# A new hand-written order for the first 24 steps of chunked attention and a rational feed-forward layer

## Chip, cores and metric

The kernel runs on one core of a Trainium2 chip. The metric is the device time of one launch in microseconds (us), the median of several runs; lower is better. The engines are called as in the profile: PE is TensorE (matmul), DVE is VectorE, ACT is ScalarE, POOL is GpSimd, SP is the queue that issues the transfers.

## The reference

Attention within chunks of 64 positions (8 batches, 8 heads, 576 positions, head width 64), whose output, read as 4608 tokens of width 512, goes through a feed-forward layer with a rational function between its two products.

```python
scores = scale * np.matmul(q_c, k_c.transpose(0, 1, 2, 4, 3))     # chunks of 64
scores = scores - np.max(scores, axis=-1, keepdims=True)
attn = np.exp(scores)
attn = attn / (np.sum(attn, axis=-1, keepdims=True) + 1e-09)
x = np.matmul(attn, v_c)                                         # as (4608, 512)
h = x @ w_in                                                     # 512 -> 2048
P = a[0] + a[1] * h + a[2] * h * h + a[3] * h * h * h
Q = 1.0 + np.abs(b[0]) * np.abs(h) + np.abs(b[1]) * h * h
out = (P / (Q + 1e-6)) @ w_out                                   # 2048 -> 512
```

## The kernel before

The 4608 tokens are 18 blocks of 256. The hidden width is cut into four parts of 512, so each block has four steps. Step g (0 to 71) is one part of one block: steps 0 to 7 alternate between blocks 0 and 1 (the weights of a part are used twice as soon as they are there), step 8 opens block 2, step 12 block 3, step 16 block 4, step 20 block 5. Every product keeps float32 accuracy by splitting its operands into a high and a low piece: the first feed-forward product (FF1) runs hi·hi, lo·hi and hi·lo, the second (FF2) ghi·wo_hi, ghi·wo_lo and glo·wo_hi. Weights come in as 16 pieces of 1 MB whose 8-byte words are joined and split on the chip.

Steps 0 to 23 follow the table START, a list of items written out by hand. The kernel schedules by hand: each engine and each transfer queue executes its items in exactly the order of the list, and an item that waits holds back everything behind it on its engine. From step 24 on another table, STEADY, repeats a pattern of a cheaper scheme with seven products instead of eight; it is the same before and after. An item is a letter, an index (step, block, weight piece, or sum) and sometimes a PSUM tag. The tags pa, p0, p1 and po name four pairs of PSUM banks; a tile that takes a tag waits until all readers of the tag's last tile are done.

- SP: q (queries and keys of a block; 0 and 1 in halves for block 0), k (the coefficients a and b), v (values), w (weight piece, L163; three raw buffers), t (fetch of sums).
- PE: S scores (L225), T transposes (L304), A attention times values (L225), F and f the two halves of FF1 (L352, 24 matmuls each), Z, z and y the three parts of FF2 (L428, 16 matmuls each).
- Attention elsewhere: M maximum (L261), U subtract (L267), n sum and reciprocal (L288 to L290) on DVE; E exponential (L274) on ACT; N the product of e with the reciprocal (L295) on DVE, Np the same on POOL; K copies the transposed e out of PSUM, at (L308), and X makes the high piece of x, xhi (L331), on ACT; Y the low piece xlo (L335) on DVE.
- Weight piece: s scales the high words (ACT, L182), o shifts the low words (DVE, L174; oa on ACT, L178), j joins them (DVE, L186), h rounds to the high piece (ACT, L189), d subtracts for the low piece (DVE, L196; dp on POOL).
- Rational function, old chain, on an FF1 tile ph in PSUM: a, b and c read ph on ACT (L356, L360, L364: tiles A, B, C); Q (L368, DVE), I and J (L372, L376, ACT: logarithm and exponential for the reciprocal); p and P (L380, L384, DVE) read ph again; g makes ghi (L389); H and R (L393, L397) one Newton correction; G the low piece glo (L402, DVE; Gp on POOL). B scales the coefficients once (L761).
- Newton chain, the same items with a u ahead (L460 to L508): it keeps its intermediate in the FF1 tile, and forms ghi by a copy on ACT (ue, L508) and glo on DVE or POOL (uG, uGp, L553).
- O copies a finished block out (ACT, L723) and stores it in four transfers (L726). m are 56 additions on w_out for the later scheme, on POOL, two of each 14 on ACT; the last of each 14 sends the sums (tt and hh) to DRAM.

The tiles e (softmax), at and o (output) share one pair of buffers, eo. ACT and DVE never read the same FF1 tile at the same time: a reader on one engine waits for the reader on the other that stands ahead of it in the list. So P, which reads ph on DVE, waits for the a, b or c ahead of it in the list, and the next user of the tag waits for P.

Of the kernel before, what the change touches and what calls it, by code (L numbers as in the profile page):

```python
# [31 lines left out]
EXP_WIDE = (0, 1, 2, 3, 4, 5, 6, 7) + tuple(range(8, NB))  # L32

START = (
# [24 lines left out]
)  # L59
FAST = 6  # L60
CHANGE = NST * FAST
# [900 lines left out]
```

## Time and profile before

| what | us |
|---|---|
| median of 3 runs | 888.95 |
| lowest and highest | 886.86, 891.35 |
| the profiled execution | 888.25 |
| its span in the trace | 886.5 |
| PE busy in it | 844.7 (95%) |

The span is the time between the first and the last recorded instruction; the profiled execution lies 0.7 us below the median of the runs, and the trace shows only that execution.

### The profile page before, as it was taken

To read this page: it belongs to the slowest core of one execution; us is meant where nothing else is said; L and a number is where in the kernel's file an instruction comes from. 1 tells how busy PE (TensorE), PEld (TensorE's weight loads), DVE (VectorE), ACT (ScalarE), POOL (GpSimd) and SP (SyncE) were. 2 spreads that over 40 slices of the span, in tenths; PEclk is the share of its full clock that TensorE was granted. 3 is DMA by queue.
4 is the path that set the end of the run, shared out by engine and by line. 5 is a ranking of instruction groups with operands and counts; after the bars stand their busy time and mean duration, and the time that the engine had idled before them with its cause. 6 is when DMAs were issued, how large, how long until landed. Compare 5 with 4: busy or idle time off the path is not lost.

```text
span 886.5 us, 20984 instructions
## 1 busy us (share of the span) xinstructions
PE 844.7 (95%) x9084; PEld 834.5 (94%) x9084; DVE 742.9 (84%) x646; ACT 536.4 (61%) x539; POOL 526.3 (59%) x325
## 2 busy tenths in 40 slices
PE   1798989999999999999999999999999999999997
PEld 1798989999999999999999999999999999999996
DVE  6897987798969987888888888888888889887785
ACT  3787774556564755665656565666656556556562
POOL 3231423523643577777777776767676768675771
PEclk9998999999999999999999999999999999999999
DMA  6752531103305335575767676767677777765861
GB/s 231 291 211 88 184 102 58 27 1 96 121 1 192 121 125 198 183 250 187 252 217 245 218 249 222 252 216 252 223 244 232 238 238 235 232 222 170 281 209 35
DMA packets 125468, 162.85 MB, mean 184 GB/s; under 512 B 6848, under 2 KB 111296, under 8 KB 122304
## 3 DMA queue, kind: packets, MB, share of 16 engines
q1 hardware_dynamic: 125216, 161.25, 55.5%
q8 instruction: 71, 1.16, 0.5%
q10 hardware_dynamic: 160, 0.26, 0.1%
q14 instruction: 21, 0.17, 0.1%
HBM read 142.61 MB, written 18.87 MB: 182 GB/s over the span
## 4 chain that ended last, share of the span: by engine, by line
PE 77%; DVE 9%; ACT 5%; DMA 4%; issue 3%; POOL 1%; SPq 0%; DVEq 0%; ACTq 0%; POOLq 0%
PE ph L352 37%; PE acc L619 14%; PE acd L619 11%; PE po L428 10%; DMA wo<-t 2%; PE pss L225 2%; PE psx L225 2%; PE pst L304 1%; DVE C L380 1%; DMA ab<-in_b 1%; ACT A L356 1%; DVE C L384 1%; DMA raw<-in_w_out 1%; DVE B L368 1%; DVE raw L174 1%
## 5 line engine op out<-in xcount | busy, mean ns | idle before, releaser
L352 PE MATMUL ph<-xhi,wi_hi 128*128 128x256 f32 x1152 | 322.9, 280 | 0.2 <-DVE xlo L335 0.2
L352 PE MATMUL ph<-xlo,wi_hi 128*128 128x256 f32 x1152 | 321.2, 279 | 0.7 <-DVE xlo L335 0.7
L352 PE MATMUL ph<-xhi,wi_lo 128*128 128x256 f32 x1152 | 321.0, 279 | 0.0
L352 PEld LDWEIGHTS ph<-xhi,wi_hi 128*128 128x128 f32 x1152 | 217.5, 189 | 0.8 <-DVE xlo L335 0.4
L352 PEld LDWEIGHTS ph<-xlo,wi_hi 128*128 128x128 f32 x1152 | 217.3, 189 | 0.9 <-DVE xlo L335 0.9
L352 PEld LDWEIGHTS ph<-xhi,wi_lo 128*128 128x128 f32 x1152 | 217.2, 189 | 0.0
L460 ACT ACTIVATE U<-ph 128x1024 f32<-128x1024 f32 x55 | 56.5, 1028 | 171.0 <-PE ph L352 157.0
L550 POOL TENSOR_TENSOR slo<-B,shi 128x1024 fp32r<-128x1024 f32 x46 | 111.0, 2413 | 71.0 <-ACT shi L542 67.6
L469 DVE SCALAR_TENSOR_TENSOR U<-U,co 128x1024 f32<-128x1024 f32 x55 | 90.7, 1648 | 26.3 <-ACT U L460 25.5
L490 DVE SCALAR_TENSOR_TENSOR U<-U,co,ph 128x1024 f32<-128x1024 f32 x55 | 69.4, 1262 | 43.1 <-ACT ph L486 43.0
L526 POOL TENSOR_TENSOR B<-C 128x512 f32<-128x512 f32 x46 | 70.8, 1539 | 55.2 <-DVE C L498 38.2
L428 PE MATMUL po<-wo,ghi 128*128 128x256 f32 (+2 forms) x768 | 97.2, 283 | 5.1 <-DVE wo L196 4.2
L428 PEld LDWEIGHTS po<-wo,ghi 128*128 128x128 f32 x768 | 93.3, 192 | 5.8 <-DVE wo L196 4.4
L518 POOL TENSOR_TENSOR graw<-C,graw 128x768 fp32r<-128x768 f32 x46 | 85.4, 1856 | 2.0 <-PE pst L304 1.3
L619 PE MATMUL acc<-wo,graw 128*128 128x256 f32 x552 | 80.3, 281 | 0.0
L482 ACT ACTIVATE B<-U,cst,co 128x1024 f32<-128x1024 f32 x55 | 68.4, 1244 | 18.3 <-DVE U L469 18.2
L498 DVE SCALAR_TENSOR_TENSOR C<-C,co,ph 128x1024 f32<-128x1024 f32 x55 | 70.4, 1280 | 1.9
L619 PEld LDWEIGHTS acc<-wo,graw 128*128 128x128 f32 x552 | 70.9, 188 | 0.7
L477 DVE SCALAR_TENSOR_TENSOR C<-C,co,ph 128x1024 f32<-128x1024 f32 x55 | 70.3, 1278 | 1.5
L486 ACT ACTIVATE ph<-B,co 128x1024 f32<-128x1024 f32 x55 | 61.6, 1120 | 15.3 <-DVE C L477 15.2
L465 ACT ACTIVATE C<-ph,co 128x1024 f32<-128x1024 f32 x55 | 66.2, 1204 | 6.9 <-PE ph L352 3.8
L494 DVE SCALAR_TENSOR_TENSOR ph<-U,ph 128x1024 f32<-128x1024 f32 x55 | 67.5, 1226 | 1.4
(105 smaller groups left out, 1658.6 us busy)
## 6 DMA issues: line engine op xcount, KB each, us to landing
wo<-t SPq DMA_DIRECT2D x90, 768.0 KB, 6.6
wo<-t SPq DMA_DIRECT2D x98, 256.0 KB, 3.3
out<-o SPq DMA_DIRECT2D x68, 128.0 KB, 6.1
raw<-in_w_in SPq DMA_DIRECT2D x8, 1024.0 KB, 6.7
raw<-in_w_out SPq DMA_DIRECT2D x8, 1024.0 KB, 6.0
v<-in_vP SPq DMA_DIRECT2D x20, 256.0 KB, 7.5
qk<-in_qT SPq DMA_DIRECT2D x36, 128.0 KB, 6.9
qk<-in_kT SPq DMA_DIRECT2D x36, 128.0 KB, 6.6
```

The lines of the kernel that those rows point to most:

```text
L352: nc.tensor.matmul(ph[:, fi, :], w[:, cc, f], x[:, cc, :], start=(k == 0), stop=(k == len(mm) - 1))
L428: nc.tensor.matmul(accs[n][i][:, cols], g[:, fi, i * 128:(i + 1) * 128], w[:, FPS * s + fi, cols], start=start, stop=stop,)
L469: nc.vector.scalar_tensor_tensor(U, U, c0, U, ALU.add, ALU.mult)
L477: nc.vector.scalar_tensor_tensor(C, C, na1, h, ALU.add, ALU.mult)
L482: nc.scalar.activation(ch[key][2], ch[key][1], AF.Ln, bias=cst[:, 0:1], scale=lsc)
L490: nc.vector.scalar_tensor_tensor(V, V, kq, h, ALU.add, ALU.mult)
L494: nc.vector.scalar_tensor_tensor(h, V, 2.0, h, ALU.subtract, ALU.mult)
L498: nc.vector.scalar_tensor_tensor(C, C, na0, h, ALU.add, ALU.mult)
L518: nc.gpsimd.tensor_sub(lo, quads(ch[steps[g]][3])[:, :, 1:4, :], hi.bitcast(F32))
L526: nc.gpsimd.tensor_sub(S[:, 0:2], q[:, 0:1].to_broadcast([P, 2, 2, 128]), q[:, 1:3])
L550: nc.gpsimd.tensor_sub(lo, sbuf[g], hi.bitcast(F32))
L619: nc.tensor.matmul(acc[n][pair][:, bank, col:col + 256], stat, mov, start=start, stop=stop)
```

## The change

Only the table START changes; its items are the same 675 in number. It puts them in another order on all engines and alters some items:

- Steps with the Newton chain: 12, 15, 16, 17, 19, 20, 22 before; 11, 12, 15, 16, 17, 19, 20, 22, 23 after. The old chain falls from 17 to 15 steps.
- In the old chain a, b, c and p, P are put so that ph changes hands less often between ACT and DVE: over the 24 steps 45 times instead of 51.
- Softmax product N: before, blocks 0, 2 and 3 on POOL, 1, 4, 5 and 6 on DVE; after, blocks 0 and 1 on DVE, 2 to 6 on POOL.
- Weight pieces: the low words of two more pieces are shifted on ACT (10 instead of 8), so on 6 instead of 8 on DVE. The low pieces of 8, 9 and 4 move from DVE to POOL, those of 2, 3 and 12 from POOL to DVE. Piece 4 is loaded ahead of the first queries instead of behind them.
- glo: Newton chain 5 on DVE and 4 on POOL (3 and 4 before), old chain 7 and 8 (8 and 9 before).

```diff
-    "q0.0 q0.1 S0.0:p0 w3 M0.0 S0.1 U0.0 E0.0 M0.1 U0.1 n0.0 w4 w0 s3 E0.1 v0 w1 Np0.0 o3 j3 h3 s4 n0.1 T0.0:pa s0 q1 "
-    "o4 j4 o0 j0 Np0.1 h4 h0 K0.0 T0.1 K0.1 d4 w5 k0 s1 d0 o1 A0.0:p0 A0.1 X0.0 X0.1 dp3 S1:p1 w2 w6 w12 v1 j1 Y0.1 "
...
+    "w4 q0.0 o4 S0.0:p1 q0.1 w3 w0 S0.1 s4 j4 M0.1 U0.1 M0.0 U0.0 v0 w1 h4 q1 E0.1 E0.0 s3 dp4 s0 oa0 n0.1 o3 w2 n0.0 "
+    "j3 N0.0 N0.1 T0.0:pa T0.1 j0 h3 d3 w5 K0.0 K0.1 o1 A0.1:p1 A0.0 h0 s1 d0 j1 X0.1 X0.0 Y0.1 Y0.0 h1 k0 S1:po w6 "
```

ACT at the very start, before (raw3 is weight piece 3, e0 and at0 belong to block 0; L189 is h, L182 is s, L308 is K):

```order
L182 ACTIVATE raw3_108<-raw3_108 128x1024
L274 ACTIVATE e0_128<-e0_128 128x512
L189 CAST wi_hi_69<-raw3_108 128x4x256
L182 ACTIVATE raw4_136<-raw4_136 128x1024
L182 ACTIVATE raw0_138<-raw0_138 128x1024
L189 CAST wo_71<-raw4_136 128x1024
L189 CAST wi_hi_69<-raw0_138 128x4x256
L308 COPY at0_171<-pst0_154 128x512 x2
```

The same place after:

```order
L182 ACTIVATE raw4_85<-raw4_85 128x1024
L189 CAST wo_71<-raw4_85 128x1024
L274 ACTIVATE e0_135<-e0_135 128x512 x2
L182 ACTIVATE raw3_111<-raw3_111 128x1024
L182 ACTIVATE raw0_113<-raw0_113 128x1024
L178 ACTIVATE raw0_113<-raw0_113,cst_75 128x1024
L189 CAST wi_hi_69<-raw3_111 128x4x256
L308 COPY at0_180<-pst0_166 128x512 x2
L189 CAST wi_hi_69<-raw0_113 128x4x256
```

The copies K of block 0 (L308) stood behind the rounding of pieces 4 and 0 (two L189); now piece 4 is rounded before the exponentials, and piece 0 behind the copies.

DVE around step 0, before (A0_0, B0_0, C0_0 and ph0_0 are step 0; e1 and xlo1 block 1's):

```order
L196 TENSOR_TENSOR wo_71<-raw5_179,wo_71 128x1024
L174 TENSOR_SCALAR raw2_257<-raw2_257 128x1024
L295 TENSOR_TENSOR e1_275<-e1_275,sm1_272 128x2x8x64
L174 TENSOR_SCALAR raw6_259<-raw6_259 128x1024
L186 SCALAR_TENSOR_TENSOR raw2_257<-raw2_257 128x1024
L368 SCALAR_TENSOR_TENSOR B0_0_338<-B0_0_338,ab_74,A0_0_336 128x1024
L186 SCALAR_TENSOR_TENSOR raw6_259<-raw6_259 128x1024
L380 TENSOR_TENSOR C0_0_341<-C0_0_341,ph0_0_282 128x1024
L384 SCALAR_TENSOR_TENSOR C0_0_341<-C0_0_341,ab_74,ph0_0_282 128x1024
```

The same place after:

```order
L174 TENSOR_SCALAR raw6_263<-raw6_263 128x1024
L295 TENSOR_TENSOR e1_280<-e1_280,sm1_274 128x2x8x64
L196 TENSOR_TENSOR wi_lo_70<-raw2_158,wi_hi_69 128x4x256
L186 SCALAR_TENSOR_TENSOR raw6_263<-raw6_263 128x1024
L196 TENSOR_TENSOR wo_71<-raw5_178,wo_71 128x1024
L368 SCALAR_TENSOR_TENSOR B0_0_341<-B0_0_341,ab_74,A0_0_391 128x1024
L380 TENSOR_TENSOR C0_0_375<-C0_0_375,ph0_0_283 128x1024
L384 SCALAR_TENSOR_TENSOR C0_0_375<-C0_0_375,ab_74,ph0_0_283 128x1024
```

The product N of block 1 (L295) has one weight operation fewer ahead of it, and Q, p and P (L368, L380, L384) have two subtractions and a joining between them and N. The attention product A1 takes the tag p0 in the new table (po in the old), and p0 is free only when this P has read ph0_0.

POOL in the weight stage, before (wi_lo and wo are the low pieces of w_in and w_out; glo1_0 is step 1's):

```order
L196 TENSOR_TENSOR wi_lo_70<-raw2_257,wi_hi_69 128x4x256
L196 TENSOR_TENSOR wi_lo_70<-raw6_259,wi_hi_69 128x4x256
L196 TENSOR_TENSOR wo_71<-raw12_261,wo_71 128x1024
L196 TENSOR_TENSOR wi_lo_70<-raw7_307,wi_hi_69 128x4x256
L402 TENSOR_TENSOR glo1_0_785<-B1_0_603,A1_0_601 128x1024
```

The same place after:

```order
L196 TENSOR_TENSOR wi_lo_70<-raw6_263,wi_hi_69 128x4x256
L196 TENSOR_TENSOR wi_lo_70<-raw7_265,wi_hi_69 128x4x256
L196 TENSOR_TENSOR wo_71<-raw9_269,wo_71 128x1024
L196 TENSOR_TENSOR wo_71<-raw8_278,wo_71 128x1024
L196 TENSOR_TENSOR wi_lo_70<-raw11_389,wi_hi_69 128x4x256
```

The low pieces of weights 9 and 8 now stand on POOL, behind that of piece 7; step 1's glo and the pieces 2 and 12 have left that stretch for DVE.

## Rows read from the trace of the kernel before

**Rows 1.** The page, its part 1: busy us, share, instructions.
```profile
PE 844.7 (95%) x9084; PEld 834.5 (94%) x9084; DVE 742.9 (84%) x646; ACT 536.4 (61%) x539; POOL 526.3 (59%) x325
```

**Rows 2.** Windows of 50 us: length, busy us of each engine, PE clock, DMA.
```profile
0.00:50.00 50.00, 25.91 (x375) 24.04 (x376) 38.76 (x42) 30.53 (x34) 14.84 (x15) 0.97 0.68 259
50.00:100.00 50.00, 45.77 (x378) 45.57 (x378) 43.62 (x40) 40.31 (x38) 14.83 (x5) 0.93 0.39 141
100.00:150.00 50.00, 47.41 (x569) 46.56 (x568) 39.42 (x35) 33.99 (x32) 14.18 (x5) 1.00 0.30 107
150.00:200.00 50.00, 47.98 (x506) 47.16 (x505) 41.99 (x39) 25.54 (x30) 18.97 (x12) 0.97 0.10 22
200.00:250.00 50.00, 49.14 (x530) 48.68 (x529) 44.34 (x36) 29.45 (x28) 27.02 (x16) 1.00 0.29 96
250.00:300.00 50.00, 50.00 (x535) 49.61 (x535) 40.63 (x34) 28.41 (x27) 21.90 (x14) 1.00 0.24 86
```

**Rows 3.** Timeline of PE: start us, us, what, idle before and its releaser.
```profile
12.67 1.11 PE L304 MATMUL pst<-ident,e 128*128 128x128 f32 x4 [4.61 <-POOL e L295]
23.25 1.09 PE L304 MATMUL pst<-ident,e 128*128 128x128 f32 x4 [9.47 <-ACT at L308]
...
28.99 0.58 PE L352 MATMUL ph<-xhi,wi_hi 128*128 128x256 f32 x1
...
38.87 1.94 PE L304 MATMUL pst<-ident,e 128*128 128x128 f32 x8 [2.67 <-DVE e L295]
...
85.24 7.67 PE L428 MATMUL po<-wo,ghi 128*128 128x256 f32 x46 [4.23 <-DVE wo L196]
...
128.12 1.16 PE L225 MATMUL pss<-qk 64*64 64x64 f32 x64 [2.33 <-DVE C L384]
...
154.32 1.54 PE L304 MATMUL pst<-ident,e 128*128 128x128 f32 x8 [2.02 <-DVE C L384]
...
218.52 2.11 PE L428 MATMUL po<-wo,ghi 128*128 128x280 f32 x16 [0.86 <-ACT ghi L508]
```

**Rows 4.** Windows just behind two of these waits, columns as in rows 2.
```profile
85.24:89.90 4.66, 4.66 (x22) 4.66 (x23) 4.62 (x5) 3.55 (x4) 2.30 (x1) 0.50 0.61 225
154.75:158.16 3.41, 3.41 (x72) 2.96 (x71) 3.15 (x3) 2.21 (x3) 3.33 (x3) 0.50 0.19 43
```

**Rows 5.** The chain that ended last: start, us, a run of FF2 matmuls.
```profile
244.09 7.54 PE po L428 x64
```

**Rows 6.** Timeline of ACT near the copies of block 0.
```profile
21.45 1.17 ACT L189 CAST wi_hi<-raw 128x1024 fp32r<-128x1024 f32 x1 [3.02 <-DVE raw L186]
22.47 0.64 ACT L308 COPY at<-pst 128x512 f32<-128x512 f32 x1
24.38 0.59 ACT L308 COPY at<-pst 128x512 f32<-128x512 f32 x1 [1.27 <-PE pst L304]
```

**Rows 7.** Timeline of DVE: two shifts, the end of step 0's chain, a low piece.
```profile
17.19 2.89 DVE L174 TENSOR_SCALAR raw<-raw 128x1024 int32<-128x1024 int32 x1
...
36.90 0.68 DVE L174 TENSOR_SCALAR raw<-raw 128x1024 int32<-128x1024 int32 x1
...
43.95 1.28 DVE L384 SCALAR_TENSOR_TENSOR C<-C,ab,ph 128x1024 f32<-128x1024 f32 x1
...
83.97 1.22 DVE L196 TENSOR_TENSOR wo<-raw,wo 128x1024 fp32r<-128x1024 f32 x1
```

**Rows 8.** Groups by line of 0 to 350 us: busy us, mean ns, idle before.
```profile
L380 DVE TENSOR_TENSOR C<-C,ph 128x1024 f32<-128x1024 f32 x17 | 20.5, 1213 | 18.5 <-ACT A L356 9.6 <-ACT B L360 8.9
...
L196 POOL TENSOR_TENSOR wo<-raw,wo 128x1024 fp32r<-128x1024 f32 x3 | 8.3, 2765 | 13.9 <-ACT wo L189 13.9
```

**Rows 9.** Timeline of ACT: the copy out O0, and block 3's K held by its stores.
```profile
155.95 1.01 ACT L723 COPY o<-po 128x1024 f32<-128x1024 f32 x1 [4.41 <-PE pst L304]
...
161.26 1.02 ACT L308 COPY at<-pst 128x1024 f32<-128x1024 f32 x1 [1.02 <-DMA out<-o]
```

**Rows 10.** Timeline of POOL: the additions m, held by the store of tt.
```profile
279.84 2.61 POOL L575 TENSOR_TENSOR tt<-wo 128x512 f32<-128x512 f32 x2 [20.95 <-DMA t<-tt]
```

44 rows, old and new, of the table START are left out of this document.

## The prediction

> **What bounds the kernel now.** I read the page first: PE works 844.7 of 886.5 us [rows 1], and the diff alters none of its matmuls, so a gain can only come out of the 41.8 us in which PE stands still, and out of matmuls that ran at half clock. The windows of 50 us say where the idle time is: 50 minus PE's busy time is 24.1, 4.2, 2.6, 2.0 and 0.9 us in the first five and nothing in the sixth [rows 2]. The reader should see that all of it lies in the stretch that START orders, and that DVE, ACT and POOL are never full there on average; single waits count, not loads. Since PE is full from 250 us on, whatever the start gains or loses is carried to the end.
>
> PE's timeline then names the waits. Ahead of the first FF1 matmul (F0, at 28.99 us) the big one is 9.47 us at T0.1, which needs a PSUM tile that the copy K0.0 has to read first; behind F0 there are six of note: 2.67 (T1, for the softmax product of block 1 on DVE), 4.23 (Z2, the FF2 of step 2, for the low piece of weight 8), 2.33 (S3, whose tag waits for a P, L384), 2.02 (T3, the same with another P) and 0.86 (z12, for a rounding on ACT) [rows 3]; two waits for xlo, 0.7 and 0.2, are left out of the sum below, since they may stay.
>
> Behind two of these waits the trace shows a granted clock of 0.50, the lower of the two levels (1.2 against 2.4 GHz) [rows 4]. FF2 matmuls at the full clock start every 7.54 / 64 = 0.118 us [rows 5]; the 22 in the 4.66 us behind Z2's wait took 0.212 each, so that stretch cost 22 × 0.094 = 2.1 us. The 3.41 us behind T3 cost about half of themselves, 1.7. Waits so cost more than their own length.
>
> **The change, part by part.** *To F0.* K0.0 at 22.47 started straight behind the rounding h0, which itself waited 3.02 for DVE's joining j0 [rows 6], behind a shift that took 2.89 us [rows 7]. In the new order both copies stand ahead of h0, and both products N0.0, N0.1 are on DVE, at about 0.7 each (512 columns, half of the 1.21 of a 1024-column operation [rows 8]). What is paid for it: piece 4 is loaded ahead of the first queries, so the second half's scores come some 1.5 to 2 us later than in the trace. From the second scores I add up DVE's operations in the new order (two maxima, two subtractions, two sums, a shift, a joining, two products: 8.3 us from about 9.5 to 10 us) and reach N0.1's end near 18, so T0.1 ends near 19.3 instead of 24.34. From T0.1's end to F0 the trace took 28.99 − 24.34 = 4.65, and K0.0, done before T0.1 there, adds its 0.64 now: 24.6; with the joining j1 ahead of Y0 25.2. **F0 3.8 us earlier** (2 if the load of piece 4 delays the scores twice as much, 5 if nothing does).
>
> *T1.* N1 has one weight operation fewer ahead of it on DVE and PE now does half of step 2 (f2) ahead of T1, so N1's end (34.6 to 35.4) meets PE's arrival at 35.2: **2.67 saved**.
>
> *A1, a new wait.* A1's tile now takes tag p0, which P0 has to leave. P0 ended at 43.95 + 1.28 = 45.23 [rows 7], 16.2 us behind F0's start. In the new order ACT has a, b and c of step 0 mixed with a rounding, a scaling and K1 (1.0 to 1.2 us each), and DVE does d2, j6 and d5 ahead of Q0, p0, P0: by those rows P0 ends at 42.7, 17.5 behind F0. PE is through with F2 at 39.0. **A wait of 3.7 us** (0 if DVE takes the two subtractions in ACT's gaps and K1 is earlier, 6 if one more DVE operation grows as the shift did). Behind it A1 and Z0 would run at the lower clock; the nearest row, Z2's stretch, says about 2.1, of which T1's own slow stretch paid some 1.5 before: **0.6 more**.
>
> *Z2.* Pieces 8 and 9 go to POOL at 2.77 us each [rows 8]; POOL has nothing else between piece 7's and piece 11's. I add up to an end near 74, and PE comes to Z2 near 79, so the cover is 5 us. On DVE, that subtraction ran at 83.97, 1.22 long [rows 7], behind step 3's P, which waited for ACT. **4.23 and the slow stretch, 2.1: 6.3 saved.** If POOL is more than 5 us late, each further microsecond is a wait at Z2.
>
> *S3 and T3.* DVE stood 18.5 us ahead of the p's for ACT's A and B, readers of the same FF1 tile [rows 8]. With 45 handovers instead of 51, and P6, P9 earlier in DVE's row than the scores and transposes need, S3's tag is free at 116.3 against PE's 117.3: **2.33 saved**. T3 and S4 are taken in the other order with other tags: **2.02 and the slow 1.7 saved, 3.7**. Step 11 as a Newton chain has as many operations as the old one on DVE and one copy (ue) that moves work from DVE to ACT, which has room [rows 2]; I cost it at nothing, as I do step 23. The cover is thin at F11 only, which needs P9 (141.2 to 141.9 against 142.8): **0.5 lost** (0 to 1).
>
> *z12.* Step 12's ghi comes earlier with the lead: **0.86 saved**.
>
> *Stores.* K3 at 161.26 waited for O0's stores, since at takes the buffer of o: O0 ended at 156.96, so four stores took 4.3 us [rows 9]. In the new order O1, O0 and E4 follow each other on the two eo buffers; adding 4.3 twice, block 4's subtraction ends near 150 and A3 wants its tile at 151.3, half a microsecond later. Stores slower by 1.8 each would make it 3.1 us of wait; **1.5 lost** (0 to 3.6).
>
> *POOL's additions m.* POOL loses products of block 0 and gets those of 4 to 6, in all no more than it idles. m stood 20.95 us for the store of its own tt [rows 10]. In the new order the queues' loads of values stand earlier, so the first store goes by 218 and Np6 ends near 275, 10 us ahead of T6. Cost nothing while this cover holds; the last m, at 304 by my count, lies ahead of START's end on PE.
>
> The Trainium skill has a rule against this part: the "GPSIMD Engine Reference", section 8 "Key points", says that GpSimd shares its SBUF interfaces with VectorE, in contention with DVE instructions in a 2-port mode or with two SBUF inputs. The trace agrees for the shift: 0.68 us alone, 2.89 while POOL subtracted [rows 7]. If the rule hit the one DVE operation beside POOL that leads to P0, it would add 2.2 us to A1's wait and make the forecast 877.2; my sum leaves it out, as bound 6 above has it.
>
> *Sum.* Saved 3.8 + 2.67 + 6.3 + 2.33 + 3.7 + 0.86 = 19.7; lost 3.7 + 0.6 + 0.5 + 1.5 = 6.3; net 13.4 us. The profiled execution took 888.25, the median is 888.95; less 13.4 they give 874.85 and 875.55. I take **875.0**.
>
> **Rivals.**
> 1. *Smaller gain, 880 to 884.* A1's wait is 6, the stores bring 3.6 and a slow stretch as behind T3 (1.7), F0 gains 2: 13.4 − 2.3 − 2.1 − 1.7 − 1.8 = 5.5, or 883. For it: the stores' time and shifts beside POOL vary in the trace. Against: four waits would have to go the bad way at once.
> 2. *No change, about 887.* The same work on ACT and DVE ends the start at the same time, and PE's waits only move. For it: DVE is busy 79 to 89% of the windows from 50 us on [rows 2]. Against: DVE waits 18.5 us at one line alone, and PE's waits are single ones.
> 3. *Slower, GpSimd becomes the bound.* Np4 to Np6 now stand in POOL's row behind the additions, up to forty of them ahead of Np6, which T6 needs at 284.7. A wait of 20.95 for tt's store as in [rows 10] ahead of it ends Np6 at 296, T6 loses 11 and the time is 886; two such waits end it at 317, T6 loses 32, and with the slow clock behind it the time is 908. Slower than before begins with Np6 later than 284.7 + 13.4 = 298. For it: POOL had such a wait in just this place. Against: the first store is issued 30 us ahead of the additions that need its buffer.
>
> **How the numbers follow.** A change of less than 0.5% (4.4 us) is about what a measurement of this kernel cannot tell from none. The forecast, 872 to 879, gets 0.62; the smaller gain 0.18; no change, POOL's single wait included, 0.12; the slower case 0.08. Faster by over 0.5%, below 884.5, is 0.80, within it 0.12, slower 0.08. For the range: if every term takes its good end (F0 5, no wait at A1, no cost of stores or F11) the net is 13.4 + 1.2 + 3.7 + 0.6 + 0.5 + 1.5 = 20.9, or 868; I start it at 869.5, and end it at 885, which takes in the smaller gain.
>
> **What would show it.** In the changed kernel's trace: F0 near 25.2; T1 without a wait; a wait of some 4 us ahead of A1, named P (L384); no wait at Z2, S3, T3 and z12; granted clock 1.00 near 79 and 146; PE full from about 205 on; Np6 ended well ahead of T6. Wrong it would be if another reader of FF1's tiles holds PE between 45 and 150 us where I found a margin of under a microsecond (T1, S3, F11, A3), if POOL's subtractions of pieces 8 and 9 end behind 79, or if the additions hold Np4 to Np6.

## The result and the profile after

The changed kernel takes **876.18 us** (median of 4 runs, 875.07 to 876.72), against 887.9 for the kernel before measured beside it; the ratio is 0.9869 with a 95% interval of 0.9838 to 0.9900. The profiled execution took 875.7, with a span of 873.9 us. The forecast was 875.0, with a range of 869.5 to 885.

The windows of the changed kernel, columns as in [rows 2]:

```profile
0.00:50.00 50.00, 28.16 (x410) 26.72 (x411) 40.19 (x48) 38.14 (x41) 9.87 (x13) 0.97 0.72 274
50.00:100.00 50.00, 50.00 (x488) 49.81 (x487) 48.20 (x42) 43.59 (x42) 17.77 (x6) 1.00 0.48 166
100.00:150.00 50.00, 47.53 (x560) 46.87 (x560) 46.54 (x39) 30.58 (x36) 16.01 (x7) 0.97 0.31 99
150.00:200.00 50.00, 49.14 (x546) 48.53 (x548) 40.38 (x35) 28.00 (x28) 16.73 (x11) 1.00 0.08 22
200.00:250.00 50.00, 50.00 (x518) 49.80 (x511) 38.77 (x33) 28.62 (x28) 31.70 (x20) 1.00 0.30 101
```

PE's idle time is now 21.8, 0, 2.5, 0.9 and 0 us, 25.2 in all against 33.8 in the same five windows of [rows 2]. DVE was busy 43.62 us of the second window there and is at 48.20 here: where PE no longer waits, DVE is now nearly full (67.7 of the 70 us between 50 and 120).

Where the lead stands once START is over is seen at one instruction that both kernels have, the first product of step 24. The list of the instructions of line 619 (minimum, median and maximum duration in ns, first and last start in us) has, for the kernel before,

```profile
L619 PE MATMUL acc<-wo,graw x552: 276/281/384, 356.1 to 865.1; 128*128 128x256 f32 x184
```

and for the changed one

```profile
L619 PE MATMUL acc<-wo,graw x552: 276/281/384, 343.1 to 852.6; 128*128 128x256 f32 x184
```

The lead is 13.0 us at that product, 12.5 at the last of them and 12.6 in the spans. What START gains is carried to the end, as the prediction said.

PE's timeline after, the rows that answer to those of [rows 3]:

```profile
17.02 1.94 PE L304 MATMUL pst<-ident,e 128*128 128x128 f32 x8 [7.27 <-DVE e L295]
...
24.75 0.39 PE L352 MATMUL ph<-xlo,wi_hi 128*128 128x256 f32 x1 [0.87 <-DVE xlo L335]
...
34.74 1.06 PE L304 MATMUL pst<-ident,e 128*128 128x128 f32 x8 [1.36 <-DVE e L295]
...
41.89 1.16 PE L225 MATMUL psx<-at,v 64*64 64x64 f32 x64 [3.25 <-DMA v<-in_vP]
...
113.90 1.06 PE L304 MATMUL pst<-ident,e 128*128 128x128 f32 x8 [2.47 <-DVE C L384]
...
154.56 1.16 PE L225 MATMUL psx<-at,v 64*64 64x64 f32 x64 [0.69 <-DVE e L267]
```

The waits at Z2, S3, T3 and z12 are gone, T1's has halved, A1's new one is there, and one that no step of the prediction had stands at T2. Behind A1 and behind T2 the granted clock was 0.56 and 0.50, all or most of the stretch at the lower level (columns as in [rows 2]):

```profile
43.30:47.20 3.90, 3.70 (x18) 3.71 (x19) 3.90 (x5) 3.90 (x5) 0.00 (x0) 0.56 0.74 303
115.50:118.40 2.90, 2.90 (x28) 2.68 (x31) 2.86 (x4) 1.66 (x2) 0.00 (x0) 0.50 0.00 0
```

The group of the p's, first of [rows 8], agrees with the fewer handovers: DVE's idle time ahead of it falls from 18.5 to 5.3 us, with 15 p's instead of 17 and a fuller DVE.

```profile
L380 DVE TENSOR_TENSOR C<-C,ph 128x1024 f32<-128x1024 f32 x15 | 18.2, 1215 | 5.3 <-ACT A L356 2.8 <-ACT C L364 2.5
```

### The profile page after: what moved, and what is told of

It is laid out like the page before. It is cut to its first block, busy times and chain, and to the rows that moved or that the text cites. A ratio compares the mean times of both kernels' runs of the same rounds, so it can differ in the third digit from the quotient of the medians.

```text
span 873.9 us, 20986 instructions
## 1 busy us (share of the span) xinstructions
PE 841.5 (96%) x9084; PEld 831.4 (95%) x9084; DVE 737.2 (84%) x644; ACT 537.7 (62%) x541; POOL 524.1 (60%) x325
## 4 chain that ended last, share of the span: by engine, by line
PE 85%; DVE 6%; DMA 5%; ACT 2%; issue 1%; SPq 1%; DVEq 0%; ACTq 0%
PE ph L352 41%; PE po L428 14%; PE acc L619 14%; PE acd L619 11%; DMA wo<-t 3%; PE psx L225 2%; PE pss L225 2%; PE pst L304 2%; DMA out<-o 1%; DVE B L368 1%; DMA raw<-in_w_out 1%; DMA Bqk<-in_kT 1%; DVE raw L186 1%; ACT U L460 0%; DVE e L267 0%
## 5 line engine op out<-in xcount | busy, mean ns | idle before, releaser
L460 ACT ACTIVATE U<-ph 128x1024 f32<-128x1024 f32 x57 | 58.6, 1027 | 164.9 <-PE ph L352 164.6
L469 DVE SCALAR_TENSOR_TENSOR U<-U,co 128x1024 f32<-128x1024 f32 x57 | 93.4, 1640 | 30.4 <-ACT U L460 29.6
L490 DVE SCALAR_TENSOR_TENSOR U<-U,co,ph 128x1024 f32<-128x1024 f32 x57 | 72.0, 1263 | 45.1 <-ACT ph L486 44.8
L526 POOL TENSOR_TENSOR B<-C 128x512 f32<-128x512 f32 x46 | 68.7, 1494 | 54.2 <-DVE C L498 37.6
L428 PE MATMUL po<-wo,ghi 128*128 128x256 f32 (+3 forms) x768 | 96.1, 284 | 0.4 <-DVE ghi L389 0.4
L482 ACT ACTIVATE B<-U,cst,co 128x1024 f32<-128x1024 f32 x57 | 70.8, 1243 | 16.0 <-DVE U L469 15.9
L486 ACT ACTIVATE ph<-B,co 128x1024 f32<-128x1024 f32 x57 | 63.8, 1120 | 18.4 <-DVE C L477 18.2
L498 DVE SCALAR_TENSOR_TENSOR C<-C,co,ph 128x1024 f32<-128x1024 f32 x57 | 73.0, 1281 | 2.0
L477 DVE SCALAR_TENSOR_TENSOR C<-C,co,ph 128x1024 f32<-128x1024 f32 x57 | 72.8, 1277 | 1.3
L494 DVE SCALAR_TENSOR_TENSOR ph<-U,ph 128x1024 f32<-128x1024 f32 x57 | 69.9, 1226 | 1.5
L473 DVE TENSOR_TENSOR C<-C,ph 128x1024 f32<-128x1024 f32 x57 | 69.0, 1210 | 2.0 <-ACT C L465 2.0
```

Of the source, the lines that this page charges most:

```text
L428: nc.tensor.matmul(accs[n][i][:, cols], g[:, fi, i * 128:(i + 1) * 128], w[:, FPS * s + fi, cols], start=start, stop=stop,)
L469: nc.vector.scalar_tensor_tensor(U, U, c0, U, ALU.add, ALU.mult)
L473: nc.vector.tensor_mul(C, C, h)
L477: nc.vector.scalar_tensor_tensor(C, C, na1, h, ALU.add, ALU.mult)
L482: nc.scalar.activation(ch[key][2], ch[key][1], AF.Ln, bias=cst[:, 0:1], scale=lsc)
L490: nc.vector.scalar_tensor_tensor(V, V, kq, h, ALU.add, ALU.mult)
```

## The experiments

The first question was whether the terms of the sum stand by themselves. Theory A says that they add up; theory B that a gain is lost at the next wait. In kernels made from the changed one all lines are one number higher (L305 is L304). Only items of START are moved; a name in a diff line is an item.

**Weights 8 and 9 on GpSimd, alone, in the kernel before.**

```diff
- ... c3 d9 a3 b5 p5 a5 F4:pa P5 d8 j11
+ ... c3 dp9 a3 b5 p5 a5 F4:pa P5 dp8 j11
```

> The kernel before with one part of the change alone: the low pieces of weights 8 and 9 on GpSimd instead of VectorE, at their old places in the list. Theory A (terms add up, as the sum of the prediction has them): Z2's wait of 4.23 us and its slow stretch of 2.1 go and the lead stays, so about 6.3 us faster, near 881.6. Theory B (the lead runs into the next wait): Z2 waits less than 1 us, but VectorE, which is the next to be waited for at T2 or S3, gains only the two subtractions, 2.4 us, so PE's wait at T2 or S3 grows from 2.3 to 4 us or more and 2 to 4 us are left, near 885.

Measured: 889.18 us against 887.32, ratio 1.0014 (0.9990 to 1.0039): nothing gained. PE's timeline has a new reason at almost the same place. Z2 is through, and Z1, which opens block 1's output in tag p1, waits for step 5's P, the last reader of that tag:

```profile
87.08 3.33 PE L428 MATMUL po<-wo,ghi 128*128 128x256 f32 x14 [3.48 <-DVE C L384]
```

The timelines of DVE and POOL show why P is late. DVE in this kernel, then the same two operations in the kernel before, then POOL in this kernel:

```profile
72.74 3.47 DVE L393 SCALAR_TENSOR_TENSOR B<-B,ghi 128x1024 f32<-128x1024 f32 x1
76.25 3.36 DVE L397 SCALAR_TENSOR_TENSOR B<-C,ab,B 128x1024 f32<-128x1024 f32 x1
```

```profile
72.55 1.22 DVE L393 SCALAR_TENSOR_TENSOR B<-B,ghi 128x1024 f32<-128x1024 f32 x1
73.81 1.28 DVE L397 SCALAR_TENSOR_TENSOR B<-C,ab,B 128x1024 f32<-128x1024 f32 x1
```

```profile
72.66 2.47 POOL L196 TENSOR_TENSOR wo<-raw,wo 128x1024 fp32r<-128x1024 f32 x1 [9.35 <-ACT wo L189]
75.73 2.79 POOL L196 TENSOR_TENSOR wo<-raw,wo 128x1024 fp32r<-128x1024 f32 x1 [0.60 <-ACT wo L189]
```

H and R of step 1 took 3.47 and 3.36 us where they had taken 1.22 and 1.28, and each ended 1.1 us behind the end of the POOL subtraction beside it (76.21 against 75.13, 79.61 against 78.52). The 2.4 us taken off DVE came back as 4.3 us of holding. ACT handed the delay on: its next c, which overwrites a tile that R reads, waited for R, and the b and a that P needs stand behind it.

```profile
79.64 1.21 ACT L364 ACTIVATE C<-ph,ab 128x1024 f32<-128x1024 f32 x1 [2.94 <-DVE B L397]
```

So the lead ran into the next wait, as theory B had it, but at Z1 instead of T2 or S3, and with nothing left of the gain.

**The same with step 1's low output product on VectorE**, in case its place behind the two subtractions on POOL was what held P.

```diff
- ... g1 H1 R1 h8 ... g3 Gp1 I5
+ ... g1 H1 R1 G1 h8 ... g3 I5
```

> The kernel before with the low pieces of weights 8 and 9 on GpSimd, as run earlier, where PE waited 3.48 us for P (L384) in place of the subtraction, and step 1's low output product moved from GpSimd, where it stood behind them, to VectorE behind step 1's last correction. If that product's place held ScalarE's next tile and so P, P comes 2 us or more earlier and the wait near 84 falls below 1.5 us. If VectorE's load or GpSimd's hold on it counts, the wait stays at 3 us or more.

Measured: a wait of 2.96 us at the same matmul, for the same P, and 893.64 us in one run. The product's place explains half a microsecond of the wait at most; it was itself held by POOL (3.29 us instead of 1.22). Why this one run took longer than the run without the move stays open.

**The same move undone in the changed kernel.**

```diff
- ... oa8 dp9 R2 ... p3 dp8 h11
+ ... oa8 d9 R2 ... p3 d8 h11
```

> The changed kernel with this part undone: the low pieces of weights 8 and 9 back on VectorE, at the places in the list where GpSimd has them. If Z2's wait was removed by the move to GpSimd, Z2 waits again, some 4 to 6 us in the trace near 75 us, with a granted clock of 0.5 behind it, T2 later by the two subtractions too, and the time is 4 to 8 us above the changed kernel's, 880 to 884. If it was removed by the new order alone (P3 and the subtraction earlier), the time stays within 1.5 us of 876.2.

Measured: 882.25 us, ratio to before 0.9946 (0.9929 to 0.9963), 6.1 us above the changed kernel's median. Z2 waits again:

```profile
82.18 2.22 PE L429 MATMUL po<-wo,ghi 128*128 128x256 f32 x10 [4.18 <-DVE wo L197]
```

So inside the new order the move is worth what the prediction gave it (6.3), and in the old order nothing. The changed kernel's rows offer a reason. There the two subtractions on POOL lie beside p and P, which read PSUM. Where one of them came while an R was running, the subtraction grew (4.09) and not R (1.28). For piece 8, POOL and DVE:

```profile
68.58 4.09 POOL L196 TENSOR_TENSOR wo<-raw,wo 128x1024 fp32r<-128x1024 f32 x1 [6.48 <-ACT wo L189]
```

```profile
70.25 1.21 DVE L380 TENSOR_TENSOR C<-C,ph 128x1024 f32<-128x1024 f32 x1
71.50 1.28 DVE L384 SCALAR_TENSOR_TENSOR C<-C,ab,ph 128x1024 f32<-128x1024 f32 x1
```

For piece 9 it is the same (POOL from 59.26 to 62.10, p 1.22 and P 1.28 between 59.67 and 62.20). No run moved the subtractions away from p and P alone, so this reason is read from rows, not tested.

**The start alone, in the kernel before.**

```diff
- ... w1 Np0.0 o3 j3 h3 s4 n0.1 T0.0:pa s0 q1 o4 j4 o0 j0 Np0.1 h4 h0 K0.0 T0.1 K0.1
+ ... w1 N0.0 o3 j3 h3 s4 n0.1 N0.1 T0.0:pa T0.1 K0.0 K0.1 s0 q1 o4 j4 o0 j0 h4 h0
```

> The kernel before with the start alone changed: both products of block 0 on VectorE, both transposes and both copies ahead of the roundings of pieces 0 and 4; everything behind as before. Theory A (terms add up): F0 starts 4 to 5 us earlier, near 24.5, and the time falls by as much, near 883.5. Theory B: F0 starts as early, but T1 still waits for the product of block 1, whose place in VectorE's row has not moved by more than 1 or 2 us, so T1's wait grows from 2.67 to 5 to 6 us and less than 2 us of the time is left, near 887.

Measured: 887.17 against 887.32 us, ratio 0.9994 (0.9974 to 1.0015). Neither theory had the reason: F0 came only 0.4 us earlier, at 28.57 instead of 28.99. PE's timeline:

```profile
26.66 1.98 PE L225 MATMUL pss<-Bqk,Aqk 64*64 64x64 f32 x64 [6.62 <-DMA Bqk<-in_kT]
28.57 0.58 PE L352 MATMUL ph<-xhi,wi_hi 128*128 128x256 f32 x1
```

S1, ahead of F0 on PE, waited 6.62 us for the keys of block 1. They stand behind weight piece 1 in SP, which was issued at 18.43 here, when a raw buffer came free. The same two loads, piece 1 and the queries that go with the keys, in SP's timeline of the kernel before and of the changed one:

```profile
19.56 0.33 SPq L163 DMA_DIRECT2D raw<-in_w_in  x1
19.93 0.43 SPq L133 DMA_DIRECT2D Aqk<-in_qT  x1
```

```profile
11.67 0.33 SPq L163 DMA_DIRECT2D raw<-in_w_in  x1
12.04 0.43 SPq L133 DMA_DIRECT2D Aqk<-in_qT  x1
```

In the kernel before, piece 1 went out when POOL had subtracted piece 3 (at 19.53, and at 18.40 in this run). In the changed kernel it goes out when POOL has subtracted piece 4, loaded first (at 11.64), 8 us earlier, and the keys behind it come earlier too.

**The keys ahead of piece 1 as well.**

```diff
- ... v0 w1 Np0.0 ...
+ ... v0 q1 w1 N0.0 ...
```

> The kernel before with the start alone changed, as run earlier, and the queries and keys of block 1 loaded ahead of weight piece 1, which held them until 18.4 us there. If that queue alone held F0, S1 does not wait and F0 starts near 24.5. If VectorE's row holds it (the low piece of x ended at 27.8, behind a shift of 2.90 us beside GpSimd), F0 starts at 27.5 to 28.5, a microsecond earlier than before at most.

Measured: 885.71 us in one run, and F0 at 28.45, now held by the low piece of x on DVE.

```profile
28.45 0.55 PE L352 MATMUL ph<-xhi,wi_hi 128*128 128x256 f32 x1 [6.20 <-DVE xlo L335]
```

The queue was one hold and DVE's row the other. Between the product of block 0's second half and the low piece of x, DVE's row still has the shift (2.90 us, beside a POOL subtraction), the joining and the subtraction of piece 4, and the shift of piece 0. The change puts the first two ahead of the first maximum and the other two on POOL and ACT. So the products, transposes and copies in their new order bring F0 half a microsecond, with the keys loaded early or not; F0's whole gain needs more of the new order.

**Steps 11 and 23 back in the old chain.**

```diff
- ... uc11 ua11 ... up11 uQ11 uP11 ... ug11 uH11 uR11 ... ue11 ... uG11
+ ... c11 a11 b11 ... p11 Q11 P11 ... g11 H11 R11 ... G11
```

> The changed kernel with steps 11 and 23 back in the old chain, item for item at the places of the Newton items. The prediction cost the two further Newton chains at nothing: within 1 us of the changed kernel's 876.2. Rival: the chain with fewer handovers of the FF1 tile is itself what took the waits at 128 to 155 us away; then waits for L384 of 2 us or more come back behind step 11, and the time is 3 us or more longer.

Measured: 876.37 us, 0.9877 (0.9845 to 0.9908), which is the changed kernel's time; no wait above 0.7 us between 120 and 160. In the trace the first product of step 24 came at 344.2, 1.1 us later than in the changed kernel, less than these times can tell from nothing. The waits of 2 us or more that the rival wanted did not come back, and costing the two chains at nothing was right as far as this run can tell.

**T2's new wait.** The changed kernel's DVE, and beside it POOL:

```profile
93.80 3.46 DVE L368 SCALAR_TENSOR_TENSOR B<-B,ab,A 128x1024 f32<-128x1024 f32 x1
...
108.38 2.92 DVE L186 SCALAR_TENSOR_TENSOR raw<-raw 128x1024 int32<-128x1024 int32 x1
...
112.47 1.28 DVE L384 SCALAR_TENSOR_TENSOR C<-C,ab,ph 128x1024 f32<-128x1024 f32 x1
113.67 2.35 DVE L368 SCALAR_TENSOR_TENSOR B<-B,ab,A 128x1024 f32<-128x1024 f32 x1
```

```profile
92.83 3.35 POOL L196 TENSOR_TENSOR wo<-raw,wo 128x1024 fp32r<-128x1024 f32 x1 [5.17 <-ACT wo L189]
107.53 2.69 POOL L295 TENSOR_TENSOR e<-e,sm 128x1024 f32<-128x1024 f32 x1 [11.35 <-DVE sm L290]
112.53 2.41 POOL L196 TENSOR_TENSOR wo<-raw,wo 128x1024 fp32r<-128x1024 f32 x1 [2.31 <-ACT wo L189]
```

Q of step 4 and the joining of piece 15 each end 1.1 us behind the end of the POOL operation beside them (97.26 against 96.18, 111.30 against 110.22), as if they had only begun then. P (L384), which reads one operand in PSUM, took its plain 1.28 beside POOL's subtraction at 112.53, and that took no longer for it (2.41). P ends at 113.75 and T2 begins at 113.90.

The two POOL operations on DVE instead:

```diff
- ... M2 D0 dp13 J4 ... n2 G4 j15 p7 y4 I7 oa14 P7 Np2 J7
+ ... M2 D0 d13 J4 ... n2 N2 G4 j15 p7 y4 I7 oa14 P7 J7
```

> The changed kernel with two GpSimd operations put on VectorE: the product of block 2 and the low piece of weight 13. They add 2.4 us to VectorE. Theory A (GpSimd holds up VectorE's operations with two operands in SBUF): step 4's Q falls from 3.46 to 1.28 us and the joining of piece 15 from 2.92 to 1.22, together 3.9, so step 7's P is 1 to 2 us earlier and T2 waits about 1 us or less. Theory B (the long operations have another cause, or VectorE's load alone counts): P is 2.4 us later and T2 waits 4 to 5 us, the time is 2.5 us or more longer.

DVE's and PE's timelines:

```profile
94.51 1.28 DVE L369 SCALAR_TENSOR_TENSOR B<-B,ab,A 128x1024 f32<-128x1024 f32 x1
...
109.35 1.22 DVE L187 SCALAR_TENSOR_TENSOR raw<-raw 128x1024 int32<-128x1024 int32 x1
...
112.94 3.21 DVE L369 SCALAR_TENSOR_TENSOR B<-B,ab,A 128x1024 f32<-128x1024 f32 x1
```

```profile
113.17 1.06 PE L305 MATMUL pst<-ident,e 128*128 128x128 f32 x8 [1.03 <-DVE C L385]
...
118.65 0.56 PE L226 MATMUL pss<-qk 64*64 64x64 f32 x22 [1.45 <-DVE C L385]
```

Both operations are back at 1.28 and 1.22 as theory A had it, though DVE has 2.4 us more to do, and T2's wait falls to 1.03. But the next Q meets the next POOL subtraction (3.21), and S3 waits 1.45: together 2.48, T2's old wait. No slow stretch follows (granted clock 1.00 from 113 to 118). Time 876.04, ratio 0.9878 (0.9861 to 0.9894): no change to be measured.

The joining of piece 15 out of the way:

```diff
- ... n2 G4 j15 p7 y4 I7 oa14 P7 Np2
+ ... n2 G4 p7 y4 I7 oa14 P7 j15 Np2
```

> The changed kernel with one VectorE operation moved three places: the joining of piece 15 behind step 7's P instead of ahead of p and P. In the changed trace it took 2.92 us beside GpSimd's product of block 2, and T2 waited 2.47 for this P. Theory A (T2's wait is that of one operation in the way): P ends near 111, T2 does not wait, no clock of 0.5 follows, S3 waits about 1.4 for step 6's P, and 2 to 3 us are gained in the trace at the first product of step 24 (343.0 in the changed kernel). Theory B (VectorE is full from 60 to 120 us and is the bound there): T2's wait goes and S3 waits 2.5 us or more instead; less than 1 us is gained.

```profile
112.64 1.04 PE L305 MATMUL pst<-ident,e 128*128 128x128 f32 x8
...
116.65 1.16 PE L226 MATMUL psx<-at,v 64*64 64x64 f32 x64 [1.14 <-ACT at L309]
118.33 0.87 PE L226 MATMUL pss<-qk 64*64 64x64 f32 x44 [0.52 <-DVE C L385]
```

In PE's timeline T2 does not wait; A2 and S3 wait 1.66 together. The first product of step 24 came at 342.0 in this kernel and 341.9 in the one above, 1.1 and 1.2 us ahead of the changed one's. Time 874.94, ratio 0.9861 (0.9845 to 0.9877), an interval that meets the changed kernel's. Of the 2 to 3 us that theory A wanted about 1.1 was kept in the trace, just above the 1 us of theory B.

**A1's wait**: values or P. First the values of block 1 alone are loaded earlier, then step 0's P is brought forward as well.

```diff
- ... w6 w7 v1 w9
+ ... w6 v1 w7 w9
```

> The changed kernel with the values of block 1 loaded ahead of weight piece 7, whose load waits for a buffer until 35.7 us and held this one until 36.2. In the changed trace A1 waited 3.25 us and the last to come were these values. If they alone held A1, its wait falls to less than 1 us. If step 0's P held it as well (the prediction's reason; it ended at 41.65, A1 began at 41.89), the wait stays at 3.0 us and now names L384.

```diff
- ... c0 T1:pa K1 d2 w11 a0 j6 F2 d5 h6 Q0 ... p0 P0 c2
+ ... c0 T1:pa a0 K1 d2 w11 j6 F2 h6 Q0 ... p0 P0 d5 c2
```

> The same load moved, and step 0's P brought forward: a ahead of the copy K1 on ScalarE, and the low piece of weight 5 behind P on VectorE. If values and P hold A1 together, P ends about 1.1 us earlier, near 40.5, and A1's wait falls to about 1.9 us; the first product of step 24 comes up to 1.1 us earlier than at 343.0, or the gain is lost at T2, where VectorE is waited for. If the copy K1 holds A1 instead, no gain.

The ends of step 0's P and the starts of A1, from DVE's and PE's timelines, with the load moved:

```profile
41.32 1.28 DVE L385 SCALAR_TENSOR_TENSOR C<-C,ab,ph 128x1024 f32<-128x1024 f32 x1
```

```profile
42.71 0.60 PE L226 MATMUL psx<-at,v 64*64 64x64 f32 x12 [3.30 <-ACT A L373]
```

and with P brought forward too:

```profile
40.33 1.28 DVE L385 SCALAR_TENSOR_TENSOR C<-C,ab,ph 128x1024 f32<-128x1024 f32 x1
```

```profile
41.71 1.56 PE L226 MATMUL psx<-at,v 64*64 64x64 f32 x48 [2.06 <-ACT B L361]
```

With the values early the wait stays at 3.30, and A1 starts 0.1 us behind P's end both times (42.60 and 42.71, 41.61 and 41.71). So P held it, as the prediction said; the ACT operations that the rows name had ended 0.9 and 1.0 us earlier. Bringing P forward took 1.2 us off, but the subtraction put behind P held step 0's ghi, and Z0 waited 1.36 for it, where it waits 0.44 in the changed kernel. One run each: 875.72 and 876.41 us.

**Four places together** (piece 15's joining behind P7, piece 13's low piece on DVE, piece 6's shift behind N1, values of block 1 ahead of piece 7).

```diff
- ... w6 w7 v1 ... n1 o6 h2 b0 B0 N1 ... D0 dp13 J4 ... j15 p7 y4 I7 oa14 P7 Np2
+ ... w6 v1 w7 ... n1 h2 b0 B0 N1 o6 ... D0 d13 J4 ... p7 y4 I7 oa14 P7 j15 Np2
```

> The changed kernel with four places moved: the joining of piece 15 behind step 7's P, the low piece of weight 13 on VectorE, the shift of piece 6 behind the product of block 1, and the values of block 1 loaded ahead of weight piece 7. Theory A (the single waits add up once the next one moves too): T1 waits less than 0.5 us, T2 not at all, step 4's Q takes 1.28 us, S3 waits less than 1 us, the first product of step 24 comes near 340.5, and the time is 873.5. Theory B (each gain runs into the next wait on VectorE): A1, S3 and A3 take up what T1 and T2 give, the first product stays at 342 to 343 and the time within 1 us of 876.

```profile
35.18 1.06 PE L305 MATMUL pst<-ident,e 128*128 128x128 f32 x8 [1.37 <-DVE e L296]
...
113.16 1.04 PE L305 MATMUL pst<-ident,e 128*128 128x128 f32 x8
...
117.83 1.16 PE L226 MATMUL pss<-qk 64*64 64x64 f32 x64 [0.52 <-DVE C L385]
```

Measured: 872.87 us (872.2 to 875.51, 5 runs), ratio to before 0.9838 (0.9816 to 0.9861). It is the fastest of all, though its interval meets the changed kernel's. T2 and S3 did as theory A had it; T1 still waits 1.37, which the moved shift was to take away, and the first product came at 342.0, not near 340.5, in the profiled execution, the longest of the five.

**The slower rival.** The product of block 6 put behind the long wait on POOL.

```diff
- ... Gp18 Np6 uH20 T6:p0 ... f23 m42 m43
+ ... Gp18 uH20 T6:p0 ... f23 m42 Np6 m43
```

> The changed kernel with the product of block 6 (on GpSimd) put behind four more of the additions: behind the wait of 24.22 us for the store of their sums, which stood behind it. It makes the slower rival come true: the product ends near 312 instead of 281.5, T6, which began at 288.1, waits 20 to 25 us, and the time grows by as much, to 897 to 901, if PE has nothing to make up for it; less than 5 us more if T6 has other cover.

Measured in one run: 877.58 us. This run does not decide it. The list is also the order of the program, so T6, which now stands ahead of the product, took block 6's exponentials undivided and waited for nothing. Its trace shows only the first half of the rival: behind a wait of 28.65 us on POOL the product ended at 313.68. That T6 would lose as much was not tested; what the changed kernel's trace says of it is below.

## Why the prediction was right, and where only its sum was

The direction and the size came out: 13.4 us forecast, 13.0 at the first product of step 24. Its terms did less well, and that the misses nearly cancel is luck. By the items below F0 gave 0.8 more and its faster matmuls 1.1 (estimated), T1 1.4 less, A1 with Z0 behind it cost 0.5 less, F11 and the stores 1.1 less, the waits for xlo that the sum left out (0.9) went, and T2 cost 3.9 that no term had: 12.5 instead of 13.4. (The prediction speaks of six waits behind F0 and names five; the trace before has no sixth above 0.73.)

- *F0.* Forecast 3.8 earlier; F0's first matmul came at 23.50 instead of 28.99, but had to wait for xlo; the first with xlo came at 24.75 instead of 29.37, 4.6 earlier. The slow first matmuls vanished (in the kernel before 12 of them started 0.21 us apart, where 0.12 is the full pace, some 1.1 us by estimate; the profile gives a granted clock of 1.00 for that stretch, so why they were slow stays open). The failed part is the price of loading piece 4 first. I counted it as a loss of 1.5 to 2 us on the scores, which it was (the second half's at 8.62 instead of 6.92); it also brings the first free buffer at 11.6 instead of 19.5 us, and the start alone without it gains nothing. No run undid F0's part in the changed kernel, so its 4.6 is read from the trace.
- *T1.* Forecast 2.67 saved, measured 1.3. The product ended at 34.60, as I had it (34.6 to 35.4); PE was there at 33.38 instead of 35.2, because F0 came earlier and ran at full pace.
- *A1.* Forecast 3.7, measured 3.25, for the reason given, with the values of block 1 as close behind: that transfer was missing from the argument. The stretch at the lower clock behind it is there as well (the 16 matmuls of Z0 took 3.50 us, 1.6 more than at the full pace, where 2.1 was forecast; Z0 itself waited 0.44).
- *Z2.* Forecast 6.3 saved; the wait and the slow stretch are gone, and undoing the move costs 6.1. What the prediction did not see is that this is a property of the whole order: alone the move gives 1.0014. Its row is also misread in one point: the P ahead of the old subtraction was step 5's, not step 3's.
- *S3 and T3.* Both waits went (2.33, and T3's 2.02 with its slow stretch). That the new places of P6 and P9 did it, and not another part of the order, is read from the trace; no run put them back. But a wait of 2.47 with 2.9 us at half clock, some 1.4 of cost, stands at T2 instead. This is the step that failed: I took S3's gain from P6 being earlier than S3 needs it and did not ask whether P7 was early enough for T2, where PE now arrives at 111.43 instead of 121.76. In the changed kernel DVE is nearly full there, and of a relief at T2 more than half comes back as waits at A2 and S3.
- *GpSimd beside VectorE.* The sum left out that a DVE operation beside a POOL one grows, and named one, 2.2 us longer ahead of A1, as the price. None grew there; Q of step 4 was 2.2 longer and the joining of piece 15 1.7, and taking the POOL operations away brought both back. The Trainium skill names this contention in the "GPSIMD Engine Reference", section 8 "Key points". The Trainium skill's page "SBUF — State Buffer", section "Who interferes with whom", says it in full: DVE instructions with two SBUF inputs and GpSimd instructions that read SBUF exclude each other, and whoever comes second waits for the whole of the other. The rows agree, in both directions and down to the P with a PSUM operand that was not held.
- *Newton chains, F11, stores, z12.* Costs forecast: 0, 0.5, 1.5, and 0.86 saved. Measured: nothing to be told from 0 (steps 11 and 23 undone), 0, 0.86 at f10 and A3 together (0.17, for K3, and 0.69; block 4's subtraction waited 3.58 us for the stores), and z12 does not wait.
- *POOL.* Np6 ended 6.6 us ahead of T6, at 281.47 against 288.08, where 10 were forecast; POOL's wait for the store of the sums fell behind it:

```profile
279.56 1.91 POOL L295 TENSOR_TENSOR e<-e,sm 128x1024 f32<-128x1024 f32 x1
281.42 1.30 POOL L578 TENSOR_TENSOR tt<-tt,hh 128x512 f32<-128x512 f32 x1
306.95 1.31 POOL L575 TENSOR_TENSOR tt<-wo 128x512 f32<-128x512 f32 x1 [24.22 <-DMA t<-tt]
```

By these rows one addition more ahead of Np6 would do no harm, and two would have put it behind a wait of 24 us, as the run above did. That such a wait costs its own length stays argued, not shown.

## What to carry to other kernels

A wait read from a trace says what can be gained there, not what will be. Before it goes into a sum, ask at the next wait whether its releaser moves as well: here two single parts of a change worth 11.7 us were worth nothing alone. Where an operation on one engine was seen to hold one on another, as here, count a move between the two with what it holds up, by looking at which operations of the first will lie beside it. And an early load is priced by when it gives its buffer back, too.

## What the runs showed of the hardware that was not expected

Beside GpSimd's elementwise operations, DVE operations took up to 2.25 us longer: 3.46 instead of 1.28 for an operation with both tensors in SBUF (back to 1.28 when the GpSimd one was taken away), 2.92 instead of 1.22, 3.47 instead of 1.22. It goes the other way as well: the GpSimd subtraction at 68.58, which came while DVE had such an operation in hand (67.91 to 69.19, the next to 70.33), took 4.09 us, and the one at 112.53, beside a P, 2.41. The p's and P's, which read their second tensor from PSUM, were not held: one took 1.28 beside a GpSimd operation that began 0.06 us later, and the mean of the 15 p's is 1215 ns in the changed kernel against 1213 before. And the release that a row names for a wait can be a bystander: with the values loaded early, A1's wait was put down to two different ACT operations, which had ended 0.9 and 1.0 us before, while its end followed step 0's P by 0.1 us in both kernels.
